# Band matrix by masked shifts, PSUM banks as one pool, and a job order by virtual time per batch, in a convolution and token-mixing kernel

## The chip, the cores and the metric

The kernel runs on one core of a Trainium2 chip. The metric is the device time of one execution in microseconds (us). The kernel before takes 223.04 us (median of 3 runs, 222.84 to 223.64). Executions of one kernel mostly agree within about 1%; some have a slower clock of the matrix engine, and only fast runs are compared here. Every profile belongs to one of these executions; its span is 1.7 to 2.1 us shorter than the time of that same execution, and differs by a few microseconds from the median.

Engines are named as in the profile: PE is the matrix engine, PEld its weight loads (which overlap with matmuls), DVE the vector engine, ACT the scalar engine, POOL the general-purpose engine that here also issues the loads of x, and SP the engine that issues the loads of the weights and the stores. PSUM is the memory that matmuls write to: 8 banks of 2 KB per partition.

## The reference, cut to what matters

```python
# x: [8, 4224, 192] f32, weight: [8 heads, 7 taps]; w_q, w_k: [192, 64]; w_out: [192, 192]
w = softmax(weight, axis=-1)                     # 7 taps per head, 24 channels per head
y[b, s, h, g] = sum_k w[h, k] * x[b, s + k - 6, h, g]     # causal, zeros before the start
wq, wk = y @ w_q, y @ w_k
W_tok  = (wq @ wk.T) / sqrt(64)                  # [4224, 4224] per batch, without softmax
mixed  = W_tok @ y
out    = relu(mixed) @ w_out                     # float32
```

There is no softmax over the tokens, so `W_tok @ y = wq @ (wk.T @ y) * scale`. Both kernels therefore never build `W_tok`. They need the Gram matrix `y.T @ y` (192 x 192), multiply it by `w_k` to a small matrix M, and apply `relu((y w_q) M)`.

## The kernel before: the parts that matter here

Each batch consists of small *jobs*. A job takes one or two PSUM banks, issues some matmuls, and is then emptied ("evacuated") by ACT or DVE into SBUF.

- Y: the convolution. For every head and half of the chunks one matmul of a 128 x 128 *band matrix* with a window of x.
- T: transposes of Y, into a ring of tiles YT. Q: `y w_q`, from YT.
- G: the Gram matrix, accumulated over 18 chunks of Y in bank 7 for the whole batch.
- MC: the chain of each batch after its last G: copy the Gram matrix out (GS), one transpose (TR), multiply by `w_k` (MM) and get M.
- Z: `relu(Q M)`, as ZD (two halves) and ZS (the third part). O: `Z w_out`, evacuated to an output buffer and stored.

The program is static: when it is built, a loop with a small clock model chooses which job PE issues next. The model has a time at which each engine and each bank becomes free. The lines that the change and the argument touch:

```python
XW  = sbuf("xw", [128, B, SLOTS, D], BF16)       # x: one slot for each of the 8 batches
YT  = sbuf("yt", [128, 3, 3, 488], BF16)         # ring of 3 transposed tiles
OUT = sbuf("o_sb", [128, 4, 2, 4 * D], F32)      # ring of 4 output buffers
...
# the band: masks by POOL, 7 products and 4 sums on DVE, then copies to the diagonal blocks
for q in range(4):
    ... e.affine_select(MASK[32*q : 32*q+32], ...)            # POOL, after the first x loads
for k in range(KC):
    ... e.tensor_tensor(TMP[:, k], MASK[:, k] (broadcast), W_S[:, :, k] (broadcast), ALU.mult)
...
# 22 memsets and casts (all but one for the weights) on POOL, and only then the x loads of batches 1 to 7
for b in range(1, B):
    load(b, 0, 0, 1, xg[b][0], [z_first, z_short])
    ...
# streams in order of priority
streams = {"MC": ..., "O": ..., "ZD": ..., "ZS": ..., "Q": ..., "T": ..., "Y": ..., "G": ...}
doubles = [[0, 0.0, []], [2, 0.0, []], [4, 0.0, []]]   # three pairs of banks: Y, T, ZD, O
single  = [[6, 0.0, []]]                               # one bank: Q, ZS, TR, MM, remainder O
...
while True:
    ...
        t = ready(streams[s][head[s]])
        key = (max(t, free["pe"] + 0.03), pr)          # earliest start; ties go to the priority
```

So the order is *eager*: whichever job can start first is taken, and the priority only decides ties. A pair of banks is filled by one job and emptied by one engine: in one instruction for ZD and O, in two or three for Y and T.

## Time and profile before

| what | value | read from |
|---|---|---|
| median time; time and span of the profiled execution | 223.04 us; 221.34 us, 219.6 us | runs, page |
| first real matmul (Y) | 14.76 us | timeline |
| last G matmul | 171.2 us | instructions of tile Y |
| last matmul | 214.4 us | windows |
| PE work of one batch at full clock | 21.1 us, so 169 us for eight | distances in the timeline |

The last row is the floor that the argument needs. A busy PE in the profile is not a full PE, because pipelined matmuls overlap. The start-to-start distances are the honest measure: 12 transposes of 122 columns took 0.64 us, one Y matmul of 432 columns 0.183 us. This is the rule in the Trainium skill, "TensorE: Matmul & The Clock Gate", section "Wait — 56ns, not 53.3ns?": columns over 2.4 GHz plus about 2.5 ns. This trace agrees (122 columns: 53.3 ns by the rule, 53.3 ns measured).

The page of the kernel before: busy time per engine, then the span in 40 slices of 5.5 us, each digit the busy tenths of PE and, below it, the granted PE clock in tenths.

```profile
span 219.6 us, 4228 instructions
PE 185.0 (84%) x1701; PEld 130.5 (59%) x1720; DVE 130.5 (59%) x244; ACT 127.1 (58%) x238; POOL 52.3 (24%) x92
...
PE   7637966999999989998999969999999679667570
PEclk9965899999999999999999999999999999999998
```

PE is the busiest engine, but it has two weak stretches: the first seven slices, with a reduced clock in slices 3 to 5, and the last nine.

The five largest waits of PE of the kernel before (line, what it waited for: us in total, times, longest). L406 is Y, L616 is O, L490 is Q, L578 is ZD:

```profile
PE ps L406 <- ACT band L326: 5.8, 1, 5.8
PE ps L406 <- DMA xw<-in_x_dram: 5.3, 3, 2.6
PE ps L616 <- DVE zt L762: 4.2, 5, 1.3
PE ps L490 <- DVE zt L762: 2.4, 3, 0.8
PE ps L578 <- ACT qt L757: 2.0, 4, 0.7
```

The timeline of the kernel before, in parts (start, duration, engine, line, what; in brackets the idle time before it and what ended that):

```profile
9.30 2.79 DVE L288 TENSOR_TENSOR tmp<-mask,w_s 128x304 bf16<-128x304 bf16 x7 [3.89 <-POOL mask L244]
...
14.76 3.06 PE L406 MATMUL ps<-xw,band 128*128 128x432 bf16 x8 [5.78 <-ACT band L326]
...
178.88 0.38 PE L578 MATMUL ps<-qt,m_sb 128*128 128x512 bf16 x1 [0.55 <-ACT qt L757]
...
180.26 0.38 PE L490 MATMUL ps<-yt,wqa 128*128 128x488 bf16 x1 [0.79 <-DVE zt L762]
```

The windows of the kernel before (stretch, its length, then busy time and number of instructions of PE, PEld, DVE, ACT and POOL, the PE clock, the share of the DMA engines, GB/s):

```profile
14.70:22.00 7.30, 5.87 (x31) 3.38 (x32) 2.90 (x6) 2.89 (x8) 5.98 (x22) 0.50 0.63 75
...
40.00:160.00 120.00, 115.53 (x1145) 86.19 (x1156) 79.93 (x146) 82.42 (x159) 18.34 (x25) 1.00 1.00 211
...
171.40:214.40 43.00, 30.52 (x253) 19.56 (x257) 19.25 (x33) 23.41 (x35) 0.00 (x0) 1.00 0.43 163
```

Three things are to be seen. First, the band holds the first Y back until 14.76 us: DVE waited 3.9 us for masks from POOL. After the pause of 5.8 us the clock is low as well: PE runs at half rate from about 12.9 to 23.2 us. Secondly, the middle is good: 1,145 matmuls in 120 us, of about 1,206 that fit (212 per batch in 21.1 us), so 95%. Thirdly, the end is bad: after the last G, PE is busy for 30.5 us of 43. There only Q, T, Z and O of the last batches are left, and they hand over to each other through ACT and DVE with holes of 0.4 to 1.3 us.

### The profile page before, as it was taken

The page shows a single profiled execution, that of the slowest core. Times are in us where ns is not written, and L with a number is a line of the kernel's source. Part 1 is how long each engine was busy: PE and PEld are TensorE (multiplying, and loading weights), DVE is VectorE, ACT ScalarE, POOL GpSimd, SP SyncE. Part 2 cuts the span into 40 slices and gives each one's busy share as a digit, 9 for nine tenths or more (in the row PEclk, how much of TensorE's full clock was granted, in tenths as well). Part 3 has the DMA queues.
Part 4 walks back from the last instruction along what each step waited for, and adds up shares of the span by engine and source line. Part 5 has one row for each costly group of instructions (what it writes and reads, how often), then busy time and mean ns, then how long its engine had stood idle before and what let it go on. Part 6 is the DMA issues. An engine that isn't in the chain of part 4 may idle for free.

```text
span 219.6 us, 4228 instructions
## 1 busy us (share of the span) xinstructions
PE 185.0 (84%) x1701; PEld 130.5 (59%) x1720; DVE 130.5 (59%) x244; ACT 127.1 (58%) x238; POOL 52.3 (24%) x92
## 2 busy tenths in 40 slices
PE   7637966999999989998999969999999679667570
PEld 2214735776876766787668844688678446444340
DVE  6355764678678749564577428863876336634440
ACT  2023453676759759545687458874975746545550
POOL 2988999999600000000000000000000000000000
PEclk9965899999999999999999999999999999999998
DMA  1993999999999999999994340365033533362554
GB/s 27 150 160 38 105 193 189 190 193 190 225 344 298 199 342 323 193 291 289 284 214 191 136 175 3 146 246 205 0 146 143 208 100 143 151 234 66 219 207 166
DMA packets 47411, 40.20 MB, mean 183 GB/s; under 512 B 37920, under 2 KB 39200, under 8 KB 47392
## 3 DMA queue, kind: packets, MB, share of 16 engines
q0 software_dynamic: 36480, 13.63, 52.7%
q1 hardware_dynamic: 10912, 26.31, 32.6%
q8 instruction: 13, 0.21, 0.4%
q14 instruction: 6, 0.05, 0.1%
HBM read 27.60 MB, written 25.95 MB: 244 GB/s over the span
## 4 chain that ended last, share of the span: by engine, by line
PE 64%; POOL 9%; DVE 8%; DMA 7%; ACT 5%; issue 3%; POOLq 0%; ACTq 0%
PE ps L616 9%; PE ps L406 9%; PE ps L618 8%; PE ps L458 8%; PE ps L578 5%; PE ps L508 5%; PE ps L509 5%; DMA xw<-in_x_dram 4%; PE ps L490 4%; POOL xw L194 3%; DMA out_dram<-o_sb 3%; PE ps L510 3%; DVE zt L762 3%; PE ps L492 3%; PE ps L491 3%
## 5 line engine op out<-in xcount | busy, mean ns | idle before, releaser
L616 PE MATMUL ps<-wo,zt 128*128 128x192 bf16 x272 | 44.7, 246 | 7.8 <-DVE zt L762 4.2
L757 ACT COPY o_sb<-ps 128x768 f32<-128x768 f32 (+1 forms) x44 | 32.4, 740 | 27.8 <-PE ps L618 24.9
L757 DVE COPY yt<-ps 128x732 bf16<-128x732 bf16 (+1 forms) x70 | 33.5, 522 | 23.0 <-PE ps L458 23.0
L757 DVE COPY o_sb<-ps 128x768 f32<-128x768 f32 x28 | 26.8, 958 | 30.4 <-PE ps L618 22.2
L618 PE MATMUL ps<-wo,zt 128*128 128x384 bf16 x136 | 44.3, 326 | 0.0
L406 PE MATMUL ps<-xw,band 128*128 128x432 bf16 x128 | 33.4, 367 | 11.1 <-ACT band L326 5.8
L760 ACT ACTIVATE zt<-ps 128x1024 bf16<-128x1024 f32 (+2 forms) x42 | 35.0, 842 | 12.8 <-PE ps L578 12.2
L757 ACT CAST y<-ps 128x432 bf16<-128x432 f32 (+2 forms) x84 | 34.4, 484 | 11.8 <-PE ps L406 11.1
L616 PEld LDWEIGHTS ps<-wo,zt 128*128 128x128 bf16 x272 | 28.3, 113 | 17.2 <-ACT zt L760 9.3
L757 DVE CAST y<-ps 128x432 bf16<-128x432 f32 (+2 forms) x60 | 31.1, 571 | 9.8 <-PE ps L406 9.0
L508 PE MATMUL ps<-y 128*128 128x192 bf16 x144 | 33.4, 246 | 0.2
L509 PE MATMUL ps<-y 128*128 128x192 bf16 x144 | 33.4, 246 | 0.0
L510 PE MATMUL ps<-y 128*128 128x128 bf16 x144 | 31.5, 219 | 0.0
L194 POOL DMA_DIRECT2D xw<-in_x_dram x32 | 30.5, 1037 | 1.3 <-issue 1.3
L458 PEld LDWEIGHTS ps<-ident,y 122*128 122x128 bf16 (+1 forms) x432 | 27.0, 101 | 5.2 <-ACT y L757 0.2
L458 PE MATMUL ps<-ident,y 122*128 122x122 bf16 (+1 forms) x432 | 29.8, 222 | 0.1
L757 ACT CAST qt<-ps 128x488 bf16<-128x488 f32 (+1 forms) x33 | 17.1, 518 | 18.6 <-PE ps L492 18.2
L762 DVE TENSOR_SCALAR zt<-ps 128x512 bf16<-128x512 f32 (+3 forms) x38 | 22.8, 616 | 3.5 <-PE ps L596 3.4
L406 PEld LDWEIGHTS ps<-xw,band 128*128 128x128 bf16 x128 | 10.3, 101 | 20.8 <-ACT band L326 6.3
L578 PE MATMUL ps<-qt,m_sb 128*128 128x512 bf16 (+1 forms) x66 | 16.3, 334 | 2.8 <-ACT qt L757 2.0
L490 PE MATMUL ps<-yt,wqa 128*128 128x488 bf16 (+1 forms) x40 | 13.8, 345 | 5.1 <-DVE zt L762 2.4
L509 PEld LDWEIGHTS ps<-y 128*128 128x128 bf16 x144 | 14.1, 98 | 4.8 <-issue 0.2
(80 smaller groups left out, 187.9 us busy)
## 6 DMA issues: line engine op xcount, KB each, us to landing
out_dram<-o_sb SPq DMA_DIRECT2D x32, 768.0 KB, 3.5
xw<-in_x_dram POOLq DMA_DIRECT2D x24, 384.0 KB, 16.8
xw<-in_x_dram POOLq DMA_DIRECT2D x8, 432.0 KB, 16.9
out_dram<-o_sb SPq DMA_DIRECT2D x8, 96.0 KB, 3.5
xw<-in_x_dram POOLq DMA_DIRECT2D x8, 45.8 KB, 14.1
xw<-in_x_dram POOLq DMA_DIRECT2D x16, 16.5 KB, 20.1
wst<-in_moe_w_out_dram SPq DMA_DIRECT2D x1, 96.0 KB, 2.2
wst<-in_moe_w_out_dram SPq DMA_DIRECT2D x2, 48.0 KB, 4.8
```

The costliest lines, as they stand in the source:

```text
L194: return e.dma_start(XW[:, b, slot : slot + n, :], bass.AP(x_t, base, [[D, 128], [CW * D, n], [1, D]]),)
L406: last = e.matmul(PS[:, k + j, 0:432], BAND[:, h, :], rhs, start=True, stop=True)
L458: last = e.transpose(bank[:, s_ * sec + o0 : s_ * sec + o0 + m], src, IDENT[0:m, 0:m])
L508: e.matmul(PS[:, 7, 0:192], y[:, 0:128], y[:, 0:192], start=c == 0, **fl)
L509: e.matmul(PS[:, 7, 192:384], y[:, 256:384], y[:, 192:384], start=False, **fl)
L510: return e.matmul(PS[:, 7, 384:512], y[:, 128:256], y[:, 128:256], start=False, **fl)
L578: last = e.matmul(PS[:, bk + h, 0:w], M_SB[:, b % 2, 256 * h : 256 * h + 128], QT[:, b % 2, s0 : s0 + w], start=True, stop=True)
L616: e.matmul(o[:, 192 * h : 192 * h + 192], ZT[:, zr, h, cols], WO1[:, :], start=h == 0, stop=False, **kw)
L618: last = e.matmul(o[:, 0:384], ZT[:, zr, 2, cols], WO2[:, :], start=False, stop=True, **kw)
L757: last = e.copy(o, i) if eng == "act" else e.tensor_copy(o, i)
L760: last = e.activation(o, i, AF.Relu)
L762: last = e.tensor_scalar(o, i, 0.0, None, op0=ALU.max)
```

## The change

Its intent is a shorter start, PSUM banks that are held no longer than needed, and an order that keeps independent work (Y and G of the next batch) in reserve to fill the hand-overs. The diff, cut to its core and regrouped; the cuts are marked.

```diff
 # --- start ---
-    for q in range(4): ... affine_select(MASK ...)       # POOL
-    for k in range(KC): ... tensor_tensor(TMP[:, k] ...)  # DVE: 7 products, 4 sums
+    load(0, 0, 0, 1, xg[0][0], z_first); load(0, 0, 1, 8, ...); load(0, 1, 0, 9, ...)  # first on POOL
+    iotas: BITS[:, 0] = 127 - partition, BITS[:, 1] = 0..4    # POOL, two small ones
+    mask = bit j of (127 - partition), five columns, kept in PSUM bank 7
+    for j in (4, 3, 2, 1, 0):
+        s, n = 1 << j, 37 + (1 << j)
+        e.copy_predicated(SHIFT[:, :, 0:n], mask[:, j] (broadcast), SHIFT[:, :, s : s + n])   # DVE
 ...    # w_q casts go to ACT, other weight casts stay on POOL behind three DMA groups instead of one
-        for i in range(24):     # warm-up matmuls
+        for i in range(22):
 # --- buffers ---
-    XW = sbuf("xw", [128, B, SLOTS, D], BF16)
-    YT = sbuf("yt", [128, 3, 3, 488], BF16)
-    OUT = sbuf("o_sb", [128, 4, 2, 4 * D], F32)
+    XW = sbuf("xw", [128, NX, SLOTS, D], BF16)        # NX = 6
+    YT = sbuf("yt", [128, NT, 3, 2 * CW], BF16)       # NT = 10 tiles of 244 columns
+    OUT = sbuf("o_sb", [128, NO, 2, 4 * D], F32)      # NO = 8
 # --- jobs: Y, T and ZD take one bank each; a Q now reads two T tiles (6 matmuls, not 3) ---
-            ("Y", b, g, hp), 2, pe, 0.37,   ...  evacs=[(make, ("Y", b, g, hp), 864, ...)]
-            ("T", b, k), 2, pe, ...
-            ("ZD", b, i), 2, pe, 0.84e-3 * w, ...
+            ("Y", b, g, h), b + KEYS["Y"][0] + KEYS["Y"][1] * (8 * g + h) / 16, 1, pe, 0.183, ...
+            ("T", b, k), b + KEYS["T"][0] + KEYS["T"][1] * k / 9, 1, pe, 0.053 * 6, ...
+            ("ZD", b, i, h), b + KEYS["Z"][0] + KEYS["Z"][1] * (3 * i + h) / 15, 1, pe, 0.42e-3 * w, ...
 # --- banks ---
-    doubles = [[0, 0.0, []], [2, 0.0, []], [4, 0.0, []]]
-    single = [[6, 0.0, []]]
+    banks = [[0.0, []] for _ in range(8)]
+    def pick(n):                        # only O takes two neighbours
+        if n == 1: bk = min((6, 0, 1, 2, 3, 4, 5), key=lambda k: banks[k][0]) ...
+        bk = min((0, 2, 4, 1, 3, 5), key=lambda k: max(banks[k][0], banks[k + 1][0])) ...
 # --- order: virtual time, in units of batches, for the start and the slope of each kind ---
+KEYS = {"Y": (0.05, 0.38), "T": (0.24, 1.19), "Q": (0.17, 0.89), "G": (0.03, 0.98),
+        "Z": (0.71, 1.02), "O": (1.05, 0.87)}
-            key = (max(t, free["pe"] + 0.03), pr)
+            t = max(t, free["pe"] + 0.02)
+            rank = (0, job.key) if t <= free["pe"] + 0.05 else (1, t)
 ...    # ZD and ZS become one stream; the clock model gets other constants (for example
 ...    # 0.14 -> 0.10 us per ACT evacuation, 0.12 -> 0.06 us per hand-over, other x arrival times)
```

A bank's neighbours are thus no longer tied together, and among the jobs that could start now the one with the smallest virtual time wins, not the one with the highest priority.

## The prediction

This was written before anything of the change had been built or run:

> **What bounds it now.** The page has PE 84% busy, DVE 59%, ACT 58%; pipelined matmuls overlap in that. From start-to-start distances in the timeline (12 transposes in 0.64 us, an O group of 768 columns in 0.33, G 0.22, Y 0.183, Q 0.205, Z 0.213 per matmul) a batch needs 21.1 us of PE, eight need 169. This agrees with the Trainium skill, "TensorE: Matmul & The Clock Gate", "Wait — 56ns, not 53.3ns?" (columns over 2.4 GHz plus 2.5 ns each). So some 51 of the 219.6 us span are not PE work:
>
> - 14.8 us before the first real matmul (timeline: DVE waits 3.9 us for POOL's masks, makes the band until 14.3).
> - about 4 us of half clock (PEclk 0.50 in the windows 14 to 20 us, after the idle from 9.0 to 14.8).
> - 5.3 us of PE waits on x (waits view). Batch 1's loads go out at 21.7 us, behind POOL's weight casts.
> - 5.3 us after the last matmul (evacuation, store).
> - about 20 us of lost overlap, mostly late. From 40 to 160 us PE issues 192 matmuls per 20 us of about 202 possible (95%). After the last G (171.4 us) only Q, T, Z, O of two batches are left: about 29 us of work in 43 us with holes of 0.3 to 1.3 us at hand-overs (Z to O, Q to Z), because the eager priority spent the independent G and Y early.
>
> **What the change does.**
>
> 1. Band and loads. The first x load waits only for a small memset: POOL issues from about 1.5 instead of 4.2 us. Packets followed 2 us later and the first two groups took 7, so x lands near 10. The band waits for iotas behind three loads (about 5 us), then softmax 1.5, five masked copies (300 to 420 elements, estimated 2.5 to 3 us in all), copies 0.9: band near 9.5 to 10. First real matmul about 10 us: 4.5 us saved. The idle after warm-up shrinks below 2 us, so the clock should stay full: 3 us saved. Batch 1 is issued near 12 us: most of the x wait saved.
> 2. Virtual time keeps G and Y of late batches for filling the O and Z of the batch before, so only one batch of Z and O (8 us of PE, 9 us of evacuation per engine) is left after the last G, plus a 2 to 3 us GS, TR, MM chain: 10 us saved.
> 3. Single banks: any of seven serves the next job; 8 output buffers, 10 YT parts. Splitting 40 Z evacuations costs 0.16 us each (ACT: 1024 columns 1.03 us, 512 in 0.60): 6 us over two engines 60% busy, not critical.
> 4. x ring of 6: the Y that its loads wait for is long done: nothing.
>
> **Sum (estimate):** 10 + 169/0.95 = 178, + 5 store tail, + 1 to 2 drain = 194 us span; the times lie 3.4 us above the profiled span: **197 us**, range 191 to 205. Faster by over 2%: 0.97; within 2%: 0.02; slower by over 2%: 0.01.
>
> **What would show it.** First Y matmul near 10 us with PEclk at least 0.9 in all slices after 7 us; PE waits on x below 2 us; last G within 15 us of the last matmul (before: 43); PE digits 9 until the last three slices; ACT and DVE near 67%.
>
> **What would make it wrong.** Masked copies at two or more cycles per element (band past 11 us) or a clock drop in the early gap: +3 us. A static order that misjudges evacuation (its model is 10% below the trace's durations): 90% instead of 95% costs 10 us. Better filling (98%): -5 us.

## The result, and the profile after

The changed kernel takes 195.03 us (median of 4 runs, 194.81 to 195.78), against 222.94 us (222.78 to 223.64, 4 runs) for the kernel before. The ratio is 0.875, with a 95% interval of 0.872 to 0.878. Here and below, a ratio is the mean time of one kernel's fast runs over the mean of the other's of the same rounds, so it is not quite the ratio of the medians that are quoted.

The page of the changed kernel; a slice is now 4.85 us:

```profile
span 194.0 us, 4387 instructions
PE 181.9 (94%) x1799; PEld 138.3 (71%) x1814; DVE 125.5 (65%) x254; ACT 139.3 (72%) x273; POOL 46.2 (24%) x74
...
PE   7749999999999999999999999999999999999980
PEclk9988999999999999999999999999999999999999
```

All waits of PE that its waits view lists. L397 is Y, L376 the warm-up, L493 is G:

```profile
PE ps L397 <- DVE zt L371: 3.3, 1, 3.3
PE ps L376 <- DVE warm L240: 1.3, 1, 1.3
PE ps L493 <- ACT y L729: 0.7, 1, 0.7
```

Parts of its timeline:

```profile
6.45 2.75 DVE L296 COPY_PREDICATED shift<-ps,shift 128x424 bf16<-128x424 int32 x5
9.22 0.87 ACT L311 COPY band<-shift 32x256 bf16<-32x256 bf16 x2 [2.72 <-DVE shift L296]
11.34 0.30 DVE L371 MEMSET zt<- 128x288 uint32 x1
11.76 2.17 PE L397 MATMUL ps<-xw,band 128*128 128x432 bf16 x8 [3.33 <-DVE zt L371]
11.93 2.64 POOL L321 CAST wall<-wst 128x192 bf16<-128x192 f32 x7 [3.47 <-DMA wst<-in_moe_w_out_dram]
```

And its windows:

```profile
13.50:17.00 3.50, 2.80 (x25) 2.26 (x24) 0.89 (x2) 1.07 (x4) 3.25 (x8) 0.63 0.69 78
...
40.00:160.00 120.00, 119.16 (x1231) 92.88 (x1240) 81.34 (x163) 92.72 (x182) 12.02 (x17) 1.00 1.00 226
...
176.70:188.40 11.70, 11.62 (x106) 8.43 (x104) 7.09 (x15) 10.47 (x20) 0.00 (x0) 1.00 0.47 175
```

The spans can be split at three events, and the differences add up (the profiled execution before was faster than its median, so they give 25.6 us and not 27.9):

| stretch | before, us | after, us | gain, us |
|---|---|---|---|
| start to first Y | 14.76 | 11.76 | 3.0 |
| first Y to last G | 156.4 | 164.7 | −8.3 |
| last G to last matmul | 43.2 | 11.9 | 31.3 |
| last matmul to end (evacuation, store) | 5.2 | 5.6 | −0.4 |
| span | 219.6 | 194.0 | 25.6 |

The second and the third row belong together: G is now issued later, so that it fills what had been holes at the end. From the first Y to the last matmul it takes 176.7 us instead of 199.6, and 169 of that is work. The waits of the old tail (O, Q and ZD on `zt` and `qt`) are gone from the list altogether. In the middle, PE issues 1,231 matmuls in 120 us of about 1,272 that fit (224 per batch now, because Q has 27 matmuls instead of 15), so about 97% instead of 95%; a few matmul records are missing in each trace.

The evacuation of Z, by group, shows what splitting costs. Before (ACT's part, 29 of the 32 pairs of full width; columns: line, engine, operation, shapes and count, busy us and mean ns of one, idle us before them and what ended most of it):

```profile
L760 ACT ACTIVATE zt<-ps 128x1024 bf16<-128x1024 f32 x29 | 29.8, 1026 | 12.2 <-PE ps L578 12.2
```

After:

```profile
L734 DVE TENSOR_SCALAR zt<-ps 128x512 bf16<-128x512 f32 x68 | 45.5, 686 | 15.1 <-PE ps L577 5.4 <-PE ps L601 5.1 <-PE ps L562 4.5
L732 ACT ACTIVATE zt<-ps 128x512 bf16<-128x512 f32 x28 | 15.7, 614 | 0.0
```

Two half evacuations on ACT cost 1.23 us instead of 1.03, so the change spends 0.2 us more evacuation per pair there, and more still on DVE (0.69 us a half), where most halves now go. In return a bank is free after a shorter instruction, and the two halves can go to two engines. What that return is worth is not seen here; zd_paired below measures it.

### The profile page after: what moved, and what is told of

It reads as the page before. It is cut to its first block, busy times and chain, and to the rows that moved or that the text cites. A ratio compares the mean times of both kernels' runs of the same rounds, so it can differ in the third digit from the quotient of the medians.

```text
span 194.0 us, 4387 instructions
## 1 busy us (share of the span) xinstructions
PE 181.9 (94%) x1799; PEld 138.3 (71%) x1814; DVE 125.5 (65%) x254; ACT 139.3 (72%) x273; POOL 46.2 (24%) x74
## 4 chain that ended last, share of the span: by engine, by line
PE 89%; DVE 4%; POOL 2%; ACT 1%; issue 1%; POOLq 0%
PE ps L472 13%; PE ps L599 12%; PE ps L442 12%; PE ps L397 11%; PE ps L601 11%; PE ps L493 7%; PE ps L562 6%; PE ps L494 6%; PE ps L495 4%; PE ps L577 4%; DVE shift L296 1%; ACT y L729 1%; POOL xw L205 1%; PE ps L526 1%; DVE xw L369 0%
## 5 line engine op out<-in xcount | busy, mean ns | idle before, releaser
L729 ACT COPY o_sb<-ps 128x768 f32<-128x768 f32 (+1 forms) x69 | 52.7, 767 | 17.8 <-PE ps L601 15.2
L734 DVE TENSOR_SCALAR zt<-ps 128x512 bf16<-128x512 f32 (+1 forms) x77 | 47.4, 632 | 19.2 <-PE ps L562 8.4
L729 ACT CAST y<-ps 128x432 bf16<-128x432 f32 (+2 forms) x110 | 46.1, 477 | 10.1 <-PE ps L397 9.7
L599 PE MATMUL ps<-wall,zt 128*128 128x192 bf16 x272 | 44.9, 247 | 0.0
L601 PE MATMUL ps<-wall,zt 128*128 128x384 bf16 x136 | 44.3, 326 | 0.0
L397 PE MATMUL ps<-xw,band 128*128 128x432 bf16 x128 | 36.7, 351 | 3.3 <-DVE zt L371 3.3
L493 PE MATMUL ps<-y 128*128 128x192 bf16 x144 | 34.8, 249 | 1.1 <-ACT y L729 0.7
L599 PEld LDWEIGHTS ps<-wall,zt 128*128 128x128 bf16 x272 | 27.7, 113 | 10.2 <-ACT o_sb L729 2.0
L442 PEld LDWEIGHTS ps<-ident,y 122*128 122x128 bf16 (+1 forms) x432 | 27.5, 97 | 3.5
L472 PE MATMUL ps<-yt,wall 128*128 128x244 bf16 (+1 forms) x216 | 28.5, 265 | 0.3
L729 DVE CAST y<-ps 128x432 bf16<-128x432 f32 x34 | 20.4, 604 | 8.9 <-PE ps L397 8.8
L472 PEld LDWEIGHTS ps<-yt,wall 128*128 128x128 bf16 x216 | 18.2, 97 | 7.5 <-DVE yt L729 4.2
L562 PE MATMUL ps<-qt,m_sb 128*128 128x512 bf16 (+1 forms) x65 | 21.1, 333 | 0.5
L732 ACT ACTIVATE zt<-ps 128x512 bf16<-128x512 f32 (+1 forms) x43 | 19.1, 479 | 1.5 <-PE ps L562 1.5
L493 PEld LDWEIGHTS ps<-y 128*128 128x128 bf16 x144 | 14.2, 99 | 4.8 <-DVE y L729 1.4
L494 PEld LDWEIGHTS ps<-y 128*128 128x128 bf16 x144 | 14.2, 99 | 3.6
```

The costliest lines, as they stand in the source:

```text
L397: return e.matmul(PS[:, k, 0:432], BAND[:, h, :], rhs, start=True, stop=True)
L442: last = e.transpose(bank[:, o0 : o0 + m], Y[0:m, b % 2, c, first : first + 128], IDENT[0:m, 0:m],)
L472: last = e.matmul(PS[:, bk, o0 : o0 + w], wt, y[:, s_], start=s_ == 0 and j == 0, stop=s_ == 2, skip_group_check=True)
L493: e.matmul(PS[:, 7, 0:192], y[:, 0:128], y[:, 0:192], start=c == 0, **fl)
L494: e.matmul(PS[:, 7, 192:384], y[:, 256:384], y[:, 192:384], start=False, **fl)
L562: return e.matmul(PS[:, bk, 0:w], M_SB[:, b % 2, 256 * h : 256 * h + 128], QT[:, b % 2, s0 : s0 + w], start=True, stop=True)
```

## The experiments

Twelve kernels were run. All gave correct results. The theory to begin with was the prediction's: the start gives about 7 us, the order by virtual time gives about 10 us in the tail, single banks and larger buffers give little. The rival was that the banks and the small jobs carry the body's gain. Halves were run first, then single parts undone, then several undone together. The three groups of runs, on two chips, each had their own runs of the kernel before (fast medians 222.43, 222.86 and 222.61 us), so ratios are more reliable than differences of medians across groups. A caution for small differences: a half-rate stretch of the clock comes in some executions and not in others (the mean clock of the changed kernel's four runs was 0.988 to 0.996), and one is worth up to 1.7 us.

| run | median, us (range) | ratio to before (95% interval) |
|---|---|---|
| the change | 195.03 (194.81–195.78) | 0.875 (0.872–0.878) |
| start_only | 216.25 (215.38–216.81) | 0.974 (0.968–0.979) |
| body_only | 201.13 (200.56–202.01) | 0.906 (0.901–0.912) |
| old_order | 200.88 (199.27–201.17) | 0.903 (0.898–0.909) |
| fixed_banks | 199.92 (199.23–201.17) | 0.901 (0.895–0.908) |
| order_banks | 201.40 (200.44–202.75) | 0.905 (0.898–0.913) |
| paired_jobs | 206.01 (205.59–206.83) | 0.926 (0.921–0.931) |
| y_paired | 197.14 (196.08–198.21) | 0.885 (0.880–0.891) |
| zd_paired | 196.30 (196.16–197.55) | 0.883 (0.879–0.887) |
| order_banks_paired | 202.47 (201.37–203.17) | 0.909 (0.904–0.914) |
| few_buffers | 195.38 (194.78–196.40) | 0.879 (0.872–0.886) |
| late_weights | 194.39 (193.76–194.69) | 0.873 (0.868–0.878) |
| late_weights_warm | 193.93 (193.61–194.61) | 0.871 (0.868–0.874) |

### start_only and body_only: the two halves

start_only has the new start (band, load order, casts) and the old jobs, banks and order. x has a slot for every batch again.

```diff
-    NX = 6; NO = 8; YT = [128, 10, 3, 244]
+    NX = 8; NO = 4; YT = [128, 3, 3, 488]
-    (jobs, banks and order of the changed kernel)
+    (jobs, banks and order of the kernel before)
```

> The new start (band by masked shifts, x first on Pool, weight casts moved, 22 warm-up matmuls) with the old body (old order, old banks, 8 x buffers, 4 output and 3 YT buffers). Theory S (start and body add up): first Y matmul near 11.8 us instead of 14.8, half clock about 3.4 us instead of 10, PE waits on x about 0 instead of 5.3; in all 8 to 10 us off: 213 to 215 us. Rival: the old body runs G and Y far ahead anyway and has its holes at the end, which an earlier start does not shorten, so less than the 3 us shift survives: 220 us or more.

body_only is the reverse: the old masks, products, casts and 24 warm-up matmuls, with the new jobs, banks, order and buffers.

```diff
-    iotas, five copy_predicated, casts on ACT and POOL by DMA group
+    masks by affine_select, 7 products, 4 sums, casts on POOL
```

> The old start with the new body (virtual time, single-bank jobs in a pool of seven, 6 x buffers, 8 output and 10 YT buffers). Theory S (parts add up): 195 plus the 8 to 10 us of the start: 203 to 205 us, first Y at 14.8 us. Rival (the start is worth only the 3 us by which the first Y moved, the rest is hidden): 198 to 200 us.

start_only took 216.25 us, that is 6.2 us less than the 222.43 of its round; body_only took 201.13, that is 21.3 us less. The sum, 27.5 us, matches the whole gain of 27.9. So the two halves add up within the spread of the runs, and the body is worth more than three times the start. In start_only the first Y is at 10.8 us, and its tail has the holes of the kernel before: the last T comes 28 us after the last G. In body_only the first Y waits 5.2 us for the band, as before, and there are no later waits on x.

The waits on x, first of start_only and then of body_only (the longest of its three waits; the other two are not on x):

```profile
PE ps L409 <- DMA xw<-in_x_dram: 6.1, 3, 2.5
```

```profile
PE ps L406 <- ACT band L336: 5.2, 1, 5.2
```

This is not what was expected: start_only issues batch 1's loads at 15.0 us and still waits 6.1 us for x, 3.6 of them after the first Y (5.3 in the kernel before), while body_only issues them at 21.1 us, about as late as the kernel before, and waits for none. So it is the new body that takes the later waits on x away, and not the earlier loads; presumably it has other work to do in these places.

### old_order: the eager rule on the new body

```diff
-        for s in streams:
+        for pr, s in enumerate(streams):
 ...
-            rank = (0, job.key) if t <= free["pe"] + 0.05 else (1, t)
+            rank = (t, pr)
```

> The changed kernel with only the choice rule put back: earliest ready job, ties to the fixed order of kinds; banks, jobs, buffers and start as changed. Theory V (order is most of the body's gain, because it keeps G and Y of later batches to fill the holes of Z and O): 208 us or more, last G again 30 us or more ahead of the last matmul. Rival P (free choice of banks and more buffers removes the holes, whatever the order): below 200 us.

It took 200.88 us, so undoing the order costs 5.9 us. This is less than the 10 us of the prediction. In its trace the tail is not the old one: the last G is at 179.8 us, even later than with virtual time (176.5), and PE is busy for 120.00 us of the stretch from 40 to 160. What it loses lies before 30 us, where PE waits for x, and at the end, where its last matmul starts at 191.5 us; in the changed kernel the last one ends at 188.4. (The profiled execution is the fastest of its four, 199.27 us, so the trace shows only part of the 5.9 us.) Its waits on x (L397 is Y):

```profile
PE ps L397 <- DMA xw<-in_x_dram: 5.5, 2, 3.7
```

The larger of the two is the first Y; the other 1.8 us is Y of batch 1, which the eager order wants before its x has landed. The changed kernel has work of batch 0 left to do in that place.

### fixed_banks: the old split of the banks, with single-bank jobs

```diff
-            bk = min((6, 0, 1, 2, 3, 4, 5), key=lambda k: banks[k][0])
+            own = (6,) if kind in ("Q", "ZS", "TR", "MM") else (0, 1, 2, 3, 4, 5)
+            bk = min(own, key=lambda k: banks[k][0])
 ...
-        bk = min((0, 2, 4, 1, 3, 5), key=...)
+        bk = min((0, 2, 4), key=...)
```

> The changed kernel with only the banks put back to fixed classes: Q, ZS, TR and MM on bank 6 alone, Y, T and ZD singly on banks 0 to 5, O on aligned pairs. Theory V: the order still fills the holes, 195 to 199 us. Rival P (the pool is the main thing): 205 us or more, with holes before Q and ZS matmuls that wait for the one bank.

It took 199.92 us; undoing the common pool costs 4.9 us. Here too the middle is full (119.97 us of 120), and here too Y of batch 1 waits 1.2 us for x, beside the first wait:

```profile
PE ps L397 <- DMA xw<-in_x_dram: 5.4, 2, 4.2
```

### order_banks: both of the above

The edits of old_order and fixed_banks together.

> The changed kernel with both the choice rule and the fixed bank classes put back; small jobs, new buffers, new start. In the single runs each of these cost 5 to 6 us, nearly all of it before 30 us as waits for x (1.2 to 1.8 us at batch 1) and a later end. Theory A (their costs add): 205 to 207 us. Theory R (they stand in for one another: with both gone Q and ZS queue on bank 6 and nothing fills): 210 us or more, and the last G early again.

201.40 us, so 6.4 us above the change and only 0.5 us above old_order alone. The losses of 5.9 and 4.9 us do not add up. Under the eager order, with single-bank jobs, the split of the banks made no difference that these runs can tell.

### paired_jobs: Y, T and ZD as two-bank jobs again

```diff
-            ("Y", b, g, h), ..., 1, pe, 0.183, ... evacs=[(make, ("Y", b, g, h), 432, ...)]
+            ("Y", b, g, hp), ..., 2, pe, 0.366, ... evacs=[(make, ("Y", b, g, hp), 864, ...)]
-            ("T", b, k), ..., 1, pe, 0.053 * 6, ...
+            ("T", b, kk), ..., len(ks), pe, 0.053 * 6 * len(ks), ...      # a pair of T, one engine
-            ("ZD", b, i, h), ..., 1, pe, 0.42e-3 * w, ...
+            ("ZD", b, i), ..., 2, pe, 0.84e-3 * w, ... [(ZT[:, n % NZ, 0:2, 0:w], PS[:, bk : bk + 2, 0:w])]
```

> The changed kernel with Y, T and ZD put back to jobs of two banks, each emptied by one engine (Z double in one instruction), under the new order, the pool and the new buffers. Theory J (small jobs matter: a pair holds two banks for two evacuations, so PE waits): 200 us or more, PE waits before Z, O or Q. Theory N (any one of order, pool and small jobs can be put back, the others fill): 195 to 199 us, PE digits 9 from 20 us on.

This is the largest single loss: 206.01 us, 11.0 us above the change, with order and pool left as they are. The windows show that the loss is in the middle. First the changed kernel, from 40 to 180 us:

```profile
40.00:180.00 140.00, 139.03 (x1450) 109.26 (x1461) 93.29 (x186) 107.65 (x211) 12.02 (x17) 1.00 0.92 217
```

Then paired_jobs, the same stretch, and below it two of its PE waits (L582 is ZD, L620 is O):

```profile
40.00:180.00 140.00, 133.88 (x1355) 101.50 (x1365) 83.80 (x136) 103.11 (x212) 11.69 (x17) 1.00 0.88 204
```

```profile
PE ps L582 <- ACT y L750: 2.3, 6, 0.4
PE ps L620 <- DVE zt L755: 1.9, 6, 0.3
```

PE issues 95 matmuls fewer in the same 140 us, although DVE and ACT are less busy. Waits of 0.3 to 0.4 us now stand between jobs in the steady state: a job waits for an evacuation of two banks on one engine. The Trainium skill, "Perfetto Trace Analysis", section "Optimizing Scalar/DVE Operations", says: "If Scalar/Vector aren't saturated, but are causing bubbles on other engines, breaking up instructions may allow work to be completed sooner." The trace agrees: ACT and DVE are not saturated (103.11 and 83.80 us busy of 140), PE has such bubbles, and breaking the pairs up is worth 11.0 us (206.0 against 195.0 us). Further below, order_banks_paired has hardly any bubbles in its middle, and there the pairs cost little.

### y_paired and zd_paired: which of the pairs

Each has one of the three edits of paired_jobs.

> The changed kernel with only Y put back to two-bank jobs, whose two evacuations follow one another on one engine (about 1.1 us, banks held throughout). Theory H: 199 to 204 us, with PE waits before Z or O that end with a Y evacuation. Theory L: 195 to 197 us.

> The changed kernel with only ZD put back to one two-bank job and one evacuation of 1024 columns (about 1.03 us on ACT, 1.23 on DVE, instead of two of 0.6 and 0.69 that can run on both engines at once). Theory L (the length of one hand-over counts: O can only start after the longest evacuation, and two banks stay held): 198 to 202 us. Theory H (what counts is how many of the seven banks are held by pairs in all, 24 pairs of Y and T against 5 of ZD a batch): 195 to 197 us.

y_paired took 197.14 us (2.1 above the change), zd_paired 196.30 (1.3 above). Together these are 3.4 of the 11.0 us. The rest is the pairs of T or the interplay of the three; T was not run alone, so this is not separated.

### order_banks_paired: order, banks and jobs all undone

The edits of order_banks and paired_jobs together. If these three parts made the body's gain, this kernel should be near start_only (216.25 us).

> The new start and the new buffers with order, bank classes and paired jobs of Y, T and ZD all put back. Theory J (the body's gain of 21 us is these three and nothing else; single-bank jobs are the base of it: alone they took the old body from 216.3 to 201.4 us): 213 to 218 us, as start_only, with holes before Q and O again and the last G 30 us or more before the last matmul. Rival B (the new buffers and the schedule's cost constants carry part of it): 210 us or less.

It took 202.47 us: 7.4 us above the change and 13.8 us below start_only. Two conclusions follow. First, pairs cost 11.0 us under the order by virtual time with the common pool, but only about 1.1 us under the eager order with the old split of the banks (202.47 against 201.40, in different groups of runs and with overlapping intervals). Order and split were changed together here; pairs with only one of them undone were not run. Secondly, about 14 us of the body's gain lie in none of the three named parts. What this kernel still has of the change is: the YT ring of ten tiles of 244 columns instead of three of 488, eight output buffers, ZD and ZS as one stream, the remainder of O no longer tied to bank 6, and the clock model by which the loop builds the order, with its other constants and its choice of the engine that evacuates.

The traces show how the two differ, though not why. The instructions of T and of the third matmul of each G in start_only (line, count, shortest, mean and longest ns, first and last start), and its windows view of the middle:

```profile
L461 PE MATMUL ps<-ident,y x432: 214/217/314, 16.1 to 192.7; 122*128 122x122 bf16 x136, 128*128 128x128 bf16 x8
L513 PE MATMUL ps<-y x144: 218/219/219, 19.4 to 164.5; 128*128 128x128 bf16 x144
```

```profile
40.00:160.00 120.00, 116.43 (x1153) 86.39 (x1151) 81.77 (x149) 82.84 (x161) 11.68 (x17) 1.00 0.93 209
```

The same of order_banks_paired:

```profile
L456 PE MATMUL ps<-ident,y x432: 214/217/228, 14.4 to 161.7; 122*128 122x122 bf16 x136, 128*128 128x128 bf16 x8
L514 PE MATMUL ps<-y x144: 218/219/220, 14.4 to 176.1; 128*128 128x128 bf16 x144
```

```profile
40.00:160.00 120.00, 119.95 (x1251) 94.94 (x1250) 74.42 (x135) 93.97 (x181) 11.49 (x17) 1.00 0.97 224
```

In start_only T runs until 192.7 us, 28 us after the last G: T, Q, Z and O of the end hang on each other with nothing independent between them. In order_banks_paired T is done at 161.7 us, before the last G at 176.1, so T and Q of the last batch can be ready when Z needs them. T runs ahead there, and in start_only it does not. (In the changed kernel the last T starts at 178.2 us, just after the last G at 176.5.) The same holds for the other two eager kernels with ten YT tiles: the last T starts at 161.6 us in old_order and at 163.1 us in order_banks. A ring of three YT tiles, each released by its Q, would hold T back as in start_only; so would a clock model that places T late. No run separates these, so the cause stays open.

### few_buffers: smaller rings

```diff
-    NO = 8
-    NT = 10
+    NO = 4
+    NT = 6
```

> The changed kernel with 4 output buffers instead of 8 and 6 YT slots instead of 10. Theory N: 195 to 198 us. Theory W (the 8 output buffers hide the stores, which land after about 7 us while x loads fill the queues, and the YT slots let T run ahead of Q): 200 us or more, with waits of the output evacuation on the store.

195.38 us, the same as the change within the spread. The 1,799 recorded matmuls of PE come in the same order in both traces. So under the order by virtual time four output buffers and six YT tiles are enough. Six tiles of 244 columns are as many columns as three of 488, in smaller pieces. This does not settle the open cause above: that was seen under the eager order, where T runs far ahead of Q, and a small ring was not run there.

### late_weights and late_weights_warm: the start again

In the changed kernel the band was complete at about 10.1 us (9.22 + 0.87), but Y started at 11.76. The profile names a memset on DVE as what ended this wait. It could also have been x, whose load shares the DMA engines with the loads of `w_k` and `w_out`. late_weights holds those loads back until the first x has landed, and issues batch 1's loads before the weight casts on POOL:

```diff
-        wload(2 * s, 0, 128, src, 0, wd, wl[s])
+        wload(2 * s, 0, 128, src, 0, wd, wl[s], () if s == 0 else xg[0][:2])
 ...    # the same for the other two loads of each weight
+    (memsets for batches 1 to 7 and the loads of batch 1, moved ahead of the weight casts)
```

> The changed kernel with the DMAs of the K and O weights held until the first two x groups have landed, and the x loads of batch 1 ahead of the weight casts on Pool. Theory X (the first Y waits for x, which shares the queues with 256 KB of weights; that the profile names the DVE memset, which ended at 11.64 us, is a coincidence): first Y at 10.2 to 10.8 us, before those memsets end, 194 us or a little less. Rival M (the first Y waits for the late DVE memsets): first Y again at 11.7 us, no change.

late_weights_warm adds 8 warm-up matmuls, so that PE has no pause before the first Y:

```diff
-        for i in range(22):
+        for i in range(30):
```

> A version meant to beat both: late_weights with 30 instead of 22 warm-up matmuls, so that they end near 10.1 us, where the band is ready, and PE is never idle for 1.6 us or more before the first Y. Expected: no half-clock window in any run (mean clock 0.995 or more in all), 193.5 to 194.5 us, at or a little below late_weights (194.4) and 0.5 to 1 us below the changed kernel. If the clock never was a cost here, it equals late_weights.

First a wait of late_weights, and then two lines of its timeline (L407 is Y):

```profile
PE ps L407 <- ACT band L311: 1.6, 1, 1.6
```

```profile
10.15 1.63 PE L407 MATMUL ps<-xw,band 128*128 128x432 bf16 x8 [1.64 <-ACT band L311]
...
11.35 0.30 DVE L358 MEMSET zt<- 128x288 uint32 x1
```

Y now starts at 10.15 us, released by the band, while the memset ends at 11.65 us, as it did in the changed kernel (11.34 + 0.30). So the memset had not been the cause; x had: the two large loads of the first x took 8.5 and 9.2 us from issue to landing in the changed kernel and 6.7 and 7.4 us here (DMA view of the first 10 us; the second figure of each is a median of three loads). Other kept traces with the same start agree: zd_paired and fixed_banks start Y at 12.15 us, after that memset, and few_buffers at 10.87 us, before it. This fits the Trainium skill, "DMA: Bandwidth & Descriptors", section "Issuing engines are not separate DMA queues": loads issued by different engines share the same 16 DMA engines. Holding back 256 KB of weights brought the first Y forward by 1.6 us against the changed kernel's trace; over all ten traces with its start the first Y lies between 10.8 and 12.15 us. In late_weights_warm the first Y follows the warm-up almost at once:

```profile
10.14 1.63 PE L407 MATMUL ps<-xw,band 128*128 128x432 bf16 x8 [0.17 <-ACT band L311]
```

The times are 194.39 and 193.93 us, about 1 us below the change for the second. They come from other rounds, and the ratios overlap (0.871, interval 0.868 to 0.874, against 0.875, interval 0.872 to 0.878). So late_weights_warm is the best version that was run, at the change's time or a little below it; a gain is not proved. Its criterion for the clock, a mean of 0.995 or more in every run, was met in four of six (the others had 0.992).

### How the expectations fared

Theories were confirmed by paired_jobs (J), few_buffers (N), late_weights (X), order_banks_paired (B) and zd_paired (H). In start_only, body_only, old_order and fixed_banks the result fell between the two theories, and order_banks came out below both, less than the sum of its parts. y_paired (197.14 us) missed theory H, which zd_paired had met, by 2 us, and came within the spread of theory L; so neither theory of what a pair costs holds for both.

## Why the prediction was right, and where its steps were wrong

The prediction said 197.0 us with a range of 191 to 205, and a span of 194; the result is 195.03 us with a span of 194.0. The 2 us between come from the last addend: the times were taken to lie 3.4 us above the span. That figure compared a median (223.04 us) with the span of one faster execution; within one execution the difference was 1.7 us before (221.34 and 219.6) and 1.8 us after (195.78 and 194.0). The span itself agrees because its terms erred in both directions and balanced; that they balanced to within 1 us was luck.

| term of the sum | predicted, us | measured, us |
|---|---|---|
| start to first Y | 10 | 11.76 |
| first Y to last matmul | 178 | 176.7 |
| drain and store | 6 to 7 | 5.6 |

- **Start (step 1), mis-sized by 1.8 us in this trace.** The band was costed well: copies of 2.5 to 3 us predicted, 2.75 measured, band ready at about 10.1 us. What failed was "x lands near 10": the prediction took the duration of the x loads (7 us) from the kernel before and forgot that the weights' loads now run at the same time; they took 8.5 to 9.2 us. late_weights shows it.
- **Clock (step 1), wrong in part.** The prediction named at least 0.9 in all slices after 7 us. Slices 3 and 4 show 8. After a pause of 3.3 us, not the predicted 2 or less, PE ran at half rate from about 12.7 to 16.1 us, 3.4 us. Before, the half rate lasted 10.2 us. These are one and three times 3,413 ns, the free-running window that the Trainium skill states in "TensorE: Matmul & The Clock Gate", section "What's actually happening". At most half a window of work is lost, 1.7 us. late_weights with a pause of 1.6 us and few_buffers with one of 2.5 us had no such stretch, but the length of the pause alone does not decide: order_banks had one after a pause of 2.8 us and another at 29 us, after one of 2.1 us. The clock lines of few_buffers and of order_banks:

```profile
PEclk9999999999999999999999999999999999999997
```

```profile
PEclk9969987999999999999999999999999999999999
```

- **Batch 1's loads (step 1), late.** They went out at 15.3 us instead of 12, since POOL waited 3.5 us for `w_out`. It did no harm: beside the first wait, no wait on x is left. But the prediction gave the earlier loads the credit, and body_only with loads at 21.1 us has no later wait on x either: the body's order of work removes them. The criterion of under 2 us is just met: of the 3.3 us before the first Y, the 1.7 us after the band was ready (10.1 us) are a wait on x.
- **Tail (step 2), right in size and wrong in cause.** The last G came 11.9 us before the last matmul; within 15 was predicted. The step that failed is the credit: the prediction gave it to the virtual time, 10 us. With the eager rule on the new body the last G comes late as well (179.8 us, against 164.5 with the same rule on the old body in start_only), so it is not the eager rule alone that spends G early. Undoing the order costs 5.9 us, and a kernel with order, banks and jobs all undone keeps 14 us of the body's gain and a late last G (176.1 us).
- **Single banks (step 3), wrong.** The prediction called the cost of the split "not critical", which holds, but gave it no gain: it counted only what the split costs the engines that evacuate. Under the new order and pool, pairs cost 11.0 us. The step that failed is to look at the busy share of ACT and DVE (60%) and not at how long a job waits for its bank.
- **Ring of x (step 4), nothing predicted.** No Y after the first waits for x in the changed kernel. It was not undone by itself.
- **Buffers, listed under step 3.** few_buffers shows that under the new order they give nothing beyond six YT tiles and four outputs.
- **Efficiency.** 95% was predicted between the first Y and the last matmul: 169 of 176.7 us is 95.6%. The middle is better (about 97%), the start and the end are worse. ACT is at 72% and DVE at 65%, where both were expected near 67%.

In short, the total was right because the PE floor (169 us) and the fixed parts at both ends were measured well, and the filled tail was right as an outcome; that the errors of the terms cancelled was luck. What the prediction said about *which* part of the change fills the tail was not right, and for about 14 us of the body's 21 us the part is still not known.

## What to carry to other kernels

When one engine's work is known (here 169 us of matmuls), predict an overlap change from that floor plus start and drain; this needs no correct story of which part achieves the overlap, and for the same reason a good total does not confirm the story. Judge the size of a PSUM job together with the issue order: pairs of banks cost 11 us under one order and about 1 us under another (with another split of the banks), so undoing one part at a time measures how well the parts were tuned to each other and not what each is worth. Put the loads that the first matmul needs ahead of weights that are used later, and do not trust the releaser that a profile names for a wait when another candidate can have ended at about the same time.

## What the Trainium skill lacked or had wrong

- "VectorE: DVE Perf Modes" gives no cost of a predicated copy. Five of them on bf16 with an int32 mask in PSUM, the largest of 424 elements per partition, took 2.75 us.
- "TensorE: Matmul & The Clock Gate", section "Part 4: PE-mode transpose", gives only durations of a transpose (about 275 ns in a kernel). Here one lasts 217 ns, but 12 of 122 columns start within 0.64 us, 53 ns apart, like any other matmul. For a budget of PE time this spacing is what counts, and a factor of four lies between them.
- The same page's section "What's actually happening" puts the half rate after at least one idle window of about 3.4 us. Here shorter pauses of PE were followed by a half-rate window: 3.3 us in the changed kernel, 2.8 and 2.1 us in order_banks; others were not (2.5 us in few_buffers, 2.2 us in paired_jobs). After pauses of 3.5 to 4.2 us there was one window each (four traces), after 5.2 and 5.8 us three, and in start_only, with pauses of 2.5 and 2.1 us, two. The length of 3,413 ns agrees: these stretches near the start lasted 3.4, 6.8 and 10.2 us.
- "Perfetto Trace Analysis", section "Optimizing Scalar/DVE Operations", advises to break up instructions where they cause bubbles on other engines, and has no figure. Here it was worth 11.0 us under one order of jobs (206.0 to 195.0 us), where PE had such bubbles, and 1.1 us or nothing under another (202.5 to 201.4 us), where PE was busy for 119.95 us of the 120 in the middle. This bears the page's condition out.
- No page warns that the releaser named for a wait can be a coincidence. Here a memset was named for 3.3 us, but with that memset in place and 256 KB of other loads moved the wait ended at 10.15 us, 1.5 us before the memset.
